# Six places instead of four for w2 groups, and loads five groups ahead, in the last MLP quarter

## The chip, the cores and the metric

The kernel runs on one core of a Trainium2 chip. The metric is the device time of one execution in microseconds; lower is better. The core has TensorE (PE; its weight loads are shown as PEld), VectorE (DVE), ScalarE (ACT), GpSimd (POOL) and SyncE (SP). SyncE and GpSimd issue the DMAs, which all run on the core's 16 DMA engines.

## The reference

The reference computes a transformer-like block and the gradients of all its inputs but one. For x of 2048 tokens by 1024 (bf16):

```python
h = layernorm(x) * (1 + ca) + sa
x = x + ga * spectral(h)              # rfft2, times complex weights, irfft2
h = layernorm(x) * (1 + cb) + sb
y = layernorm(h)
z = y @ w1 + b1                       # 1024 x 3584
x = x + gb * (gelu(z) @ w2 + b2)      # w2: 3584 x 1024
# outputs: x, and by vjp with grad_out the gradients of
# A_x, A_w_r, A_w_i, B_w1, B_b1, B_w2, B_b2, c, w_mod
```

sa to gb are six rows of silu(c) @ w_mod. The change touches only how w2 is brought on chip for `gelu(z) @ w2` on the last 512 tokens.

## The kernel before, in words

The program goes through these stages: modulation rows and the transposed gradient gBoT; the product ph of that gradient with w2 transposed; the forward spectral stage; the MLP forward with its activation's derivative, in four quarters of 512 tokens (b = 0 to 3, some 330 to 768 us); then the pg passes (gz times w1 transposed), the layer norms backward with the gradient of w2, the backward spectral stage, and the gradient of w1.

Within a quarter two kinds of work alternate, in the order of a written list (`plan`):

- `z_block` (seven groups g per quarter, 512 hidden units each): 32 matmuls for z (L802), then ScalarE and VectorE make gelu(z), called hh, and the derivative. The derivative is multiplied into a tile `ph` that was loaded from memory (L796). The product, gz, is stored from that same tile to `d_gz` by GpSimd (L824). Two tiles take turns as `ph`, by the group's running number n: `uvp1[:, 1]` for even n and `uvp2[:, 0]` for odd n. The profile calls these tiles hhC and w2sA. The last z group has n = 27.
- `bo_pass` (two halves h of 512 output columns, seven groups g each): a bias row (L840), then 16 matmuls (L851) per group that add hh times a w2 group into four PSUM banks. The w2 group is 512 KB, and its number is n = (2b + h) * 7 + g, 0 to 55. The last quarter has groups 42 to 55. After the seventh group ScalarE empties the banks into `otile` (L860), VectorE multiplies and adds, and the half is stored to the output.

The z groups of one quarter run beside the `bo` groups of the quarter before, so the last quarter's `bo` groups have no z work beside them.

The w2 groups sit in four places, group n in `w2p[n % 4]`. By their names in the profile the four are w2sA (the second half of that tile, `uvp2[:, 1]`), w2sC, w2sD (the first half, beside the accumulator `gacc`) and w2sB. `w2_load(upto)` issues on SyncE all loads up to a number (L833). In the last quarter it is called with n + 3.

The half's store of the output, `store_tok_half`, is one plain DMA on SyncE (L155) and two indirect scatters on GpSimd (L160). `load_tok_half` brings grad_out for the half by one plain DMA (L137) and two gathers on GpSimd (L142).

While the last `bo` groups run, SyncE also issues what the pg passes need: 28 DMA transposes of w1 into `w1T` (L935) and seven loads of gz into `gzr` (L925). Both are tied behind certain w2 loads by `behind_w2(k)`, which names group 42 + k. The tiles of the next stage, n3u and n2u (L1094, L1096), reuse the memory of `uvp1` and `uvp2`.

A scheduler orders each engine's instructions when the program is built. Orders written with `ordered()` and `tc.issue_after` are kept, and the rest goes by priority and readiness as it estimates them. On the chip each queue then runs in that fixed order, with waits on semaphores. A DMA that writes a tile waits for all that still read or write that part of it.

Of the kernel before, what the change touches and what calls it, by code (L numbers as in the profile page):

```python
# [24 lines left out]
KH = D // 2  # L25
# [5 lines left out]
NB = 4  # L31
# [4 lines left out]
def kernel(  # L36
# [24 lines left out]
    nc = tc.nc  # L61
# [58 lines left out]
    def chunk_rows(dt, i):  # L120
        return dt[4 * i * P:4 * (i + 1) * P, :].rearrange("(q p) d -> p q d", p=P)
# [13 lines left out]
    def load_tok_half(t4, src, i, h):  # L135
        s3 = tok_flat(src)
        nc.sync.dma_start(out=t4[:, 0:4:3, :],  # L137
                          in_=bass.AP(tensor=s3.tensor, offset=s3.offset + 128 * i * D + h * KH, ap=[[D, P], [1024 * D, 2], [1, KH]]))
        s2 = s3.rearrange("n (h d) -> (n h) d", h=2)
        for q in range(2):  # L140
            k = 4 * i + 2 * q + h
            nc.gpsimd.indirect_dma_start(out=t4[:, 1 + q, :], out_offset=None, in_=s2,  # L142
                                         in_offset=bass.IndirectOffsetOnAxis(ap=oidx[:, k:k + 1], axis=0))
# [9 lines left out]
    def store_tok_half(dst, t4, i, h):  # L153
        s3 = tok_flat(dst)
        nc.sync.dma_start(out=bass.AP(tensor=s3.tensor, offset=s3.offset + 128 * i * D + h * KH, ap=[[D, P], [1024 * D, 2], [1, KH]]),  # L155
                          in_=t4[:, 0:4:3, :])
        s2 = s3.rearrange("n (h d) -> (n h) d", h=2)
        for q in range(2):
            k = 4 * i + 2 * q + h
            nc.gpsimd.indirect_dma_start(out=s2, out_offset=bass.IndirectOffsetOnAxis(ap=oidx[:, k:k + 1], axis=0),  # L160
                                         in_=t4[:, 1 + q, :], in_offset=None)
# [7 lines left out]
    def bcn(row, n):  # L169
        return bass.AP(tensor=row.tensor, offset=row.offset, ap=[row.ap[0], [0, n], row.ap[1]])  # L170

    def tt(out, a, b, op):
        return nc.vector.tensor_tensor(out=out, in0=a, in1=b, op=op)  # L173
# [501 lines left out]
    def ordered():  # L675
        return tc.issue_after(last_pe[0].ins)
# [84 lines left out]
    uvp1 = reg.tile([P, 2, 4, BW], BF16, name="hhC", tag="uv1")  # L761
    uvp2 = reg.tile([P, 2, 4, BW], BF16, name="w2sA", tag="uv2")
# [4 lines left out]
    w2p = [uvp2[:, 1], reg.tile([P, 4, BW], BF16, name="w2sC", tag="gm")[:], px1t[:, 0]]  # L767
# [58 lines left out]
    w2_v = B_w2.rearrange("(c p) d -> p c d", p=P)  # L826
    w2_in = []

    def w2_load(upto):
        while len(w2_in) <= min(upto, NB * 14 - 1):  # L830
            n = len(w2_in)
            h, g = n // 7 % 2, n % 7
            w2_in.append(nc.sync.dma_start(out=w2p[n % 4], in_=w2_v[:, g * 4:(g + 1) * 4, h * KH:(h + 1) * KH]))  # L833

    def bo_pass(b, h):
        cs_ = slice(h * KH, (h + 1) * KH)
        pbs = [((ps_s, ps_d)[k % 2] if (b, h) == (NB - 1, 0) else ps_f)("pbo") for k in range(4)]
        for i in range(4):
            with ordered():
                last_pe[0] = nc.tensor.matmul(pbs[i][:], lhsT=ones_bf[32 * i:32 * i + 1, :],  # L840
                                              rhs=b2_row[32 * i:32 * i + 1, cs_], start=True, stop=False,
                                              tile_position=(32 * i, 0))
        for g in range(7):
            n = (2 * b + h) * 7 + g
            w2_load(n + 3 if b == NB - 1 else n)
            wp = w2p[n % 4]
            hh = hh_slots[(b * 7 + g) % 11]
            for i in range(4):
                for k in range(4):
                    with ordered():  # L850
                        last_pe[0] = nc.tensor.matmul(pbs[i][:], lhsT=hh[:, k, i * P:(i + 1) * P], rhs=wp[:, k, :],  # L851
                                                      start=False, stop=(g == 6 and k == 3))
            if g < 6:
                yield
        bo, x1t, go = (otile[0][:, k] for k in range(3))
        nc.sync.dma_start(out=x1t, in_=chunk_rows(d_x1, b)[:, :, cs_])
        load_tok_half(go, grad_out, b, h)
        for i in range(4):
            with tc.high_priority():
                last_ev[0] = nc.scalar.copy(out=bo[:, i, :], in_=pbs[i][:])  # L860
        tt(go, go, bo, ALU.mult)
        tt(bo, bo, bcn(gb_row[:, cs_], 4), ALU.mult)
        tt(bo, bo, x1t, ALU.add)
        store_tok_half(out_0, bo, b, h)

        yield
        pa = (ps_f if (b, h) in ((NB - 2, 1), (NB - 1, 1)) else ps_d)("pa")
        for i in range(4):
            with ordered():
                last_pe[0] = nc.tensor.matmul(pa[32 * i:32 * (i + 1), :], lhsT=ones_bf[:, 0:32], rhs=go[:, i, :], start=True, stop=True)  # L870
        with tc.high_priority():
            if b == 0:
                nc.vector.tensor_copy(out=gacc[:, cs_], in_=pa[:])
            else:
                tt(gacc[:, cs_], gacc[:, cs_], pa[:], ALU.add)

    def bo_both(b):
        for h in range(2):
            late = bo_pass(b, h)
            for _ in range(7):  # L880
                next(late)
                yield
            bo_late.append(late)
# [469 lines left out]
```

## Time and profile before

| | |
|---|---|
| median of three runs | 1469.18 us (1469.07 to 1473.41) |
| the profiled execution's own time | 1474.63 us |
| its span in the profile | 1472.8 us |
| TensorE busy | 1395.1 us, 95% |
| VectorE, ScalarE, GpSimd busy | 1072.9, 717.8, 376.5 us |
| mean granted TensorE clock | 0.988 |
| DMA | 324.27 MB, mean 220 GB/s |
| last quarter's `bo` groups on TensorE | 711.8 to 768.0 us |

Busy time is what an engine's own instructions took; idle time before an instruction is shown in brackets with what ended it. SPq and POOLq rows are issues: a DMA's row there is the time that the queue took to issue it, not the transfer. A timeline row merges neighbours of one line. Where the text gives a landing, it is the last increment of that DMA's completion semaphore in the trace.

### The profile page before, as it was taken

Reading aid. Unit: us, or ns where it says so; the run is one execution under the profiler, and the core shown is the slowest. Engines: PE = TensorE matmul, PEld = TensorE weight load, DVE = VectorE, ACT = ScalarE, POOL = GpSimd, SP = SyncE. Lnnn points to the kernel's source line nnn. Section 1 sums busy time; section 2 is a strip of 40 time slices with the busy share of each in tenths; the row PEclk is TensorE's granted clock in tenths of the full one; section 3 lists DMA queues with packets and bytes.
Section 4 is the critical chain, followed back from the end, with each engine's and each line's share of the span. In section 5 each row is a group of like instructions: output and inputs, shape, how many; then the busy total and the mean of one; then the engine's idle time right before and its main releaser. Section 6 shows DMA issues by size and latency. Waiting matters only on the chain. (4 is left out here: it accounts for less than half of the span.)

```text
span 1472.8 us, 18265 instructions
## 1 busy us (share of the span) xinstructions
PE 1395.1 (95%) x6703; PEld 650.6 (44%) x6835; DVE 1072.9 (73%) x1581; ACT 717.8 (49%) x953; POOL 376.5 (26%) x441
## 2 busy tenths in 40 slices
PE   5889989999999999999989999999999999999997
PEld 2434545444444444444434444444444444444443
DVE  5984786898799788887520789888467578898542
ACT  4765545857887666665312333342622434444211
POOL 5720541211112222122211011021245431322422
PEclk9999999999999999999999999999999999999999
DMA  9982563999777776796999275396699998766993
GB/s 335 279 228 58 144 219 114 262 258 335 242 245 232 235 248 223 229 292 216 235 303 250 91 256 186 121 266 172 184 226 242 236 218 220 191 193 181 291 235 115
DMA packets 358366, 324.27 MB, mean 220 GB/s; under 512 B 209386, under 2 KB 301056, under 8 KB 358022
## 3 DMA queue, kind: packets, MB, share of 16 engines
q1 hardware_dynamic: 324166, 207.71, 52.9%
q0 software_dynamic: 34112, 115.41, 22.8%
q8 instruction: 53, 0.87, 0.2%
q14 instruction: 35, 0.29, 0.1%
HBM read 162.06 MB, written 111.20 MB: 186 GB/s over the span
## 5 line engine op out<-in xcount | busy, mean ns | idle before, releaser
L684 PE MATMUL pp<-gBoT,wt 128*128 128x512 bf16 x878 | 196.8, 381 | 5.8 <-DMA wt<-in_B_w_dram 3.2
L948 PE MATMUL pg<-w1T,gzr 128*128 128x512 bf16 x876 | 194.6, 379 | 1.6 <-ACT gn3a L956 0.2
L1252 PE MATMUL gw1acc<-gzh,n3n 128*128 128x512 bf16 x876 | 193.8, 379 | 2.3 <-DMA gzh<-d_gz 1.3
L802 PEld LDWEIGHTS <-w 128*128 128x128 bf16 x896 | 87.6, 98 | 112.5 <-issue 9.0
L684 PEld LDWEIGHTS <-wt 128*128 128x128 bf16 x896 | 87.7, 98 | 109.9 <-issue 4.2
L948 PEld LDWEIGHTS <-gzr 128*128 128x128 bf16 x896 | 86.8, 98 | 107.9 <-issue 4.9
L1252 PEld LDWEIGHTS <-n3n 128*128 128x128 bf16 x896 | 87.5, 98 | 106.1 <-issue 2.8
L802 PE MATMUL pz<-n3Ta,w 128*128 128x512 bf16 x437 | 99.4, 383 | 6.1 <-ACT gt L805 4.1
L1071 PE MATMUL gw2acc<-gB,hhsA 128*128 128x512 bf16 x438 | 99.3, 384 | 3.7 <-ACT gwo L1078 3.1
L802 PE MATMUL pz<-n3Tb,w 128*128 128x512 bf16 x439 | 98.4, 379 | 0.5
L851 PEld LDWEIGHTS <-hhA 128*128 128x128 bf16 x608 | 59.4, 98 | 77.5 <-issue 8.0
L811 ACT ACTIVATE gt<-gt 128x2048 bf16<-128x2048 bf16 x28 | 53.5, 1911 | 71.1 <-DVE gt L173 71.1
L805 ACT ACTIVATE gt<-pz,b_col 128x512 bf16<-128x512 f32 x112 | 72.8, 684 | 28.9 <-PE pz L802 26.9
L173 DVE TENSOR_TENSOR gt<-gt,gt 128x2048 bf16<-128x2048 bf16 x56 | 68.5, 1223 | 21.6 <-ACT gt L813 20.9
L1256 ACT CAST gwo<-gw1acc 128x512 bf16<-128x512 f32 x50 | 29.0, 584 | 113.0 <-PE gw1acc L1252 98.7
L1078 ACT CAST gwo<-gw2acc 128x512 bf16<-128x512 f32 x46 | 26.8, 584 | 111.7 <-PE gw2acc L1071 84.0
L173 DVE TENSOR_TENSOR ct<-ct 128x2048 bf16<-128x2048 bf16 x64 | 75.9, 1217 | 2.6 <-DMA d_n<-ct 1.8
L992 DVE CUSTOM_DVE_ANT_0 otl<-otl 128x1024 bf16<-128x1024 bf16 x24 | 29.0, 1222 | 57.5 <-DMA otl<-in_w_mod_dram 51.5
L1071 PEld LDWEIGHTS <-hhsA 128*128 128x128 bf16 x448 | 44.1, 99 | 56.4 <-DMA hhsA<-d_hh 3.6
L807 ACT ACTIVATE gt<-gt 128x2048 bf16<-128x2048 bf16 x28 | 53.4, 1908 | 0.6
L813 ACT ACTIVATE gt<-gt 128x2048 bf16<-128x2048 bf16 x28 | 53.4, 1907 | 0.5
L1257 POOL DMA_DIRECT2D out_dram<-gwo x56 | 30.9, 553 | 78.9 <-ACT gwo L1256 46.8
(317 smaller groups left out, 2520.1 us busy)
## 6 DMA issues: line engine op xcount, KB each, us to landing
gzr<-d_gz SPq DMA_DIRECT2D x28, 512.0 KB
wblk<-in_w_mod_dram SPq DMA_DIRECT2D x12, 1024.0 KB
out_dram<-otl POOLq DMA_DIRECT2D x48, 256.0 KB
out_dram<-gwo POOLq DMA_DIRECT2D x96, 128.0 KB
d_ph<-pho POOLq DMA_DIRECT2D x21, 512.0 KB
d_hh<-hhA POOLq DMA_DIRECT2D x19, 512.0 KB
w2sD<-in_B_w_dram SPq DMA_DIRECT2D x14, 512.0 KB
hhC<-d_ph SPq DMA_DIRECT2D x14, 512.0 KB
```

The costliest lines, as they stand in the source:

```text
L173: return nc.vector.tensor_tensor(out=out, in0=a, in1=b, op=op)
L684: last_pe[0] = nc.tensor.matmul(pp[:], lhsT=wt[:, fg % 2, cch, k * P:(k + 1) * P], rhs=gBoT[j][:, cch, :], start=(cch == 0), stop=(cch == ...
L802: last_pe[0] = nc.tensor.matmul(pz[:], lhsT=w1s[g][:, cch, k * P:(k + 1) * P], rhs=n3T[:, cch, :], start=(cch == 0), stop=(cch == NDC - 1))
L805: nc.scalar.activation(out=zb[:, k, :], in_=pz[:], func=ACT.Identity, bias=b1_col[:, fc:fc + 1], scale=1.0)
L807: nc.scalar.activation(out=av, in_=zb, func=ACT.Square)
L811: nc.scalar.activation(out=sg, in_=bv, func=ACT.Sigmoid, scale=2.0 * GK)
L813: nc.scalar.activation(out=bv, in_=bv, func=ACT.Sigmoid, scale=-2.0 * GK)
L851: last_pe[0] = nc.tensor.matmul(pbs[i][:], lhsT=hh[:, k, i * P:(i + 1) * P], rhs=wp[:, k, :], start=False, stop=(g == 6 and k == 3))
L948: last_pg[0] = nc.tensor.matmul(pgs[i][:], lhsT=gzs[b, g][:, k, i * P:(i + 1) * P], rhs=w1Ts[g][:, k, h * KH:(h + 1) * KH], start=(g == 0 ...
L1071: nc.tensor.matmul(acc[:], lhsT=hh_of(fc)[:, t, :], rhs=gBs[t // 4][:, t % 4, h * KH:(h + 1) * KH], start=(t == 0), stop=(t == NT - 1))
L1252: nc.tensor.matmul(acc[:], lhsT=n3ns[t // 4][:, t % 4, cch * P:(cch + 1) * P], rhs=gz2[t // 8][:, t % 8, :], start=(t == 0), stop=(t == NT ...
L1257: nc.gpsimd.dma_start(out=out_4[cch * P:(cch + 1) * P, fg * 512:(fg + 1) * 512], in_=ob)
```

## The change

From group 46 on (the fifth of the last quarter), the w2 groups go round six places instead of four: `uvp1[:, 1]`, `uvp2[:, 0]` and the four old ones in the order w2sD, w2sB, w2sA's second half, w2sC. So 46 and 52 are in hhC's second half, 47 and 53 in w2sA's first half, 48 and 54 in w2sD, 49 and 55 in w2sB, 50 in w2sA's second half, 51 in w2sC. The loads of the last quarter are called for with n + 3 up to n = 44 and with n + 5 from n = 45 on. All other lines are the same; those below the first edit have numbers higher by 8 in the changed kernel.

```diff
     w2_v = B_w2.rearrange("(c p) d -> p c d", p=P)
     w2_in = []
 
+    W2_LAST = (NB - 1) * 14 + 4
+
+    def w2_slot(n):
+        if n < W2_LAST:
+            return w2p[n % 4]
+        k = (n - W2_LAST) % 6
+        return (uvp1[:, 1], uvp2[:, 0])[k] if k < 2 else w2p[(W2_LAST + k - 2) % 4]
+
     def w2_load(upto):
         while len(w2_in) <= min(upto, NB * 14 - 1):
             n = len(w2_in)
             h, g = n // 7 % 2, n % 7
-            w2_in.append(nc.sync.dma_start(out=w2p[n % 4], in_=w2_v[:, g * 4:(g + 1) * 4, h * KH:(h + 1) * KH]))
+            w2_in.append(nc.sync.dma_start(out=w2_slot(n), in_=w2_v[:, g * 4:(g + 1) * 4, h * KH:(h + 1) * KH]))
...
         for g in range(7):
             n = (2 * b + h) * 7 + g
-            w2_load(n + 3 if b == NB - 1 else n)
-            wp = w2p[n % 4]
+            w2_load(n + (5 if n >= W2_LAST - 1 else 3) if b == NB - 1 else n)
+            wp = w2_slot(n)
             hh = hh_slots[(b * 7 + g) % 11]
```

## The prediction

> **What bounds the kernel now.** I read the page's engine line first, then TensorE's timeline in the last MLP quarter, then the queues of SyncE and GpSimd over the same stretch.
>
> ```profile
> PE 1395.1 (95%) x6703; PEld 650.6 (44%) x6835; DVE 1072.9 (73%) x1581; ACT 717.8 (49%) x953; POOL 376.5 (26%) x441
> ```
>
> TensorE is busy 95% of 1472.8 us, so a microsecond taken from or given to its in-order stream mostly reaches the end. In the timeline (start, us, engine, line, out<-in, count, idle before) the last quarter has two waits for a w2 group:
>
> ```profile
> 722.90 3.62 PE L851 MATMUL pbo<-w2sC,hhC 128*128 128x512 bf16 x16
> 726.36 3.62 PE L851 MATMUL pbo<-w2sD,hhA 128*128 128x512 bf16 x16
> 729.81 3.62 PE L851 MATMUL pbo<-w2sB,hhA 128*128 128x512 bf16 x15
> 734.19 3.61 PE L851 MATMUL pbo<-w2sA,hhA 128*128 128x512 bf16 x16 [0.76 <-DMA w2sA<-in_B_w_dram]
> ...
> 742.08 4.90 PE L851 MATMUL pbo<-w2sC,hhA 128*128 128x512 bf16 x16 [3.95 <-DMA w2sC<-in_B_w_dram]
> 746.82 3.62 PE L851 MATMUL pbo<-w2sD,hhB 128*128 128x512 bf16 x15
> ```
>
> These rows are groups 45 to 50 in order (45 starts at 722.90; 46, 47, 48, 49, 50 follow; the bias row before 49 is left out). Groups 48 and 49 wait 0.76 and 3.95 us. Group 49 also runs 4.90 us where 3.62 is usual, because the granted clock is half for 3.41 us there. The change can win 0.76 + 3.95 + 1.28 = 6.0 us, and no more: no other group of this quarter waits.
>
> Why they are late: SyncE issues the load of 48 at 724.40 and of 49 at 730.05, and they land 9.8 and 12.0 us later (last completion increment in the trace at 734.15 and 742.04), where a quiet one takes 3.6 (708.42 to 712.00). The windows (PE busy, PEld, DVE, ACT, POOL, clock, DMA share, GB/s) show all 16 DMA engines full:
>
> ```profile
> 725.00:730.00 5.00, 5.00 (x25) 2.25 (x23) 0.52 (x4) 0.00 (x0) 1.12 (x2) 1.00 1.14 195
> 730.00:735.00 5.00, 4.18 (x19) 1.84 (x19) 0.00 (x0) 0.00 (x0) 0.21 (x1) 1.00 1.17 206
> 740.00:745.00 5.00, 2.92 (x8) 1.08 (x8) 0.84 (x1) 1.07 (x2) 0.00 (x0) 0.66 1.18 265
> ```
>
> The last view is GpSimd's timeline, which the two new places bring into play:
>
> ```profile
> 710.19 0.75 POOL L824 DMA_DIRECT2D d_gz<-hhC  x1 [6.71 <-DVE gb_acc L822]
> ...
> 724.02 1.30 POOL L160 DMA_INDIRECT out_dram<-otile,xu  x1 [1.04 <-DMA out_dram<-otile]
> 725.37 0.80 POOL L824 DMA_DIRECT2D d_gz<-w2sA  x1
> 734.79 0.99 POOL L160 DMA_INDIRECT out_dram<-otile,xu  x1 [8.63 <-issue]
> ```
>
> L824 stores gz out of the two ph buffers, hhC's second half and w2sA's first half, which become the new places. The 8.63 us before the second scatter are a wait: GpSimd holds a semaphore instruction of 8.69 us there until the first scatter, issued at 724.02, has landed at 734.01 (10.0 us). Both write the output, so the second waits for the first. Whatever stands behind the second scatter in that queue waits too.
>
> **The change, part by part.**
>
> *Issuing five ahead instead of three.* The same 14 loads of 512 KB, the same matmuls; VectorE's and ScalarE's orders are unchanged, TensorE's too but for the places read. Nothing is added in work. On a DMA system that is full from 710 to 790 us, earlier loads push other transfers back: at 714 one load more is in flight than before, worth 512 KB at some 200 to 260 GB/s, 2 to 2.6 us of all other traffic.
>
> *Group 46 into hhC.* It must wait for the gz store issued at 710.19, which lands at 714.34. So it is issued at about 714.4 and lands by 720 at the neighbours' latency (4.4 to 5.4 us); it is needed at 726.4. Cost nothing; cover 6 us.
>
> *Group 47 into w2sA's first half.* This decides. That half is ph of the very last z group; VectorE finishes it at 725.1 and GpSimd stores it. In the built program the orders around it are (numbers are w2 groups, T a w1 transpose):
>
> ```
> SyncE  before: 44 T 45 T 46 T out x1 47 go T 48 T gz 49 T 50 T 51 ...
> SyncE  after:  44 T 45 46 T T 48 out x1 49 go T 50 T T gz 47 51 52 T ...
> GpSimd before: gather gather scatter1 gz-store scatter2
> GpSimd after:  gather gather scatter1 scatter2 gz-store
> ```
>
> Two steps are moved. On SyncE, 47 now stands behind 48, 49 and 50, and with it 51, 52 and the transposes stand behind 47's wait. On GpSimd the gz store has gone behind the second scatter. So 47's load hangs on a chain: scatter 1 lands, scatter 2 is issued, the gz store is issued, lands, the load is issued, lands. TensorE needs group 47 at 729.8 and its order is fixed, so all of the chain past 729.8 is idle time.
>
> The chain with this run's rows: scatter 1 is still issued at 724.0 and lands at 734.0. Scatter 2 follows at 734.8 as it did, and takes 1.0 us to issue, so the store is issued at 735.8 instead of 725.4. From 734.0 to 742.96 the software queue moved the rest of the store (4.5 us, landed at 738.50) and then scatter 2 (4.46 us); after the change it has the two in the other order, and I give them the same 8.9 us: 734.8 + 8.9 = 743.7. The store's own latency is bounded by 3.35 us (the one issued at 695.95) and 13.13 us (the one issued at 725.37); mine is 7.9, between them, by the queue it shares. SyncE has reached the wait by then: two transposes and a gz load after 724.4 took until 738.6 here (issue times of 4.31, 0.56 and 7.26 us).
>
> The load: 4.42 to 5.81 us for those issued between 738 and 749, 3.45 in a quiet stretch (673.45), 12.0 at worst (730.05). SyncE has issued nothing for some microseconds, so I take 4.5, near the lower rows. Group 47 lands at 748.2.
>
> By a formula of the Trainium skill (DMA: Bandwidth & Descriptors, Anatomy of one DMA) a 512 KB transfer takes 2.0 us plus its bytes at 436 GB/s, an estimate of 3.2 us. The quiet rows of 3.35 and 3.45 agree; the 13.13 and 12.0 of this stretch do not. By it store and load would end at 742.2 and the net cost be some 7.7 us.
>
> *Sum.* Idle before group 47: 748.2 - 729.8 = 18.4. One half-clock stretch after it: 1.3, as at 742 (the longest such stretch in the trace, 6.83 us, would cost 3.4; no idle time this long has a row). Given back: 6.0, since 48, 49 and 50 are in their places by then. Net 18.4 + 1.3 - 6.0 = +13.7 us.
>
> *What is late next.* Nothing. From 748.2 group 47 ends at 753.0, 48 at 756.5, and 51 starts at 764.1, 53 at 771, 54 at 774.4, 55 at 777.9. 51 and 52 are issued right behind 47 and land by 752. 53 to 55 find their places free at 753.0, 756.5 and 760.3, and 55 is issued at about 762, behind an output store that needs VectorE's three operations of half 0. With 6 us each, all have 9 us or more to spare. The pg pass starts at 781 instead of 768, and what it loads has had 13 us more to arrive; it did not wait before. From 768 to 1125 TensorE waits for no DMA, only for VectorE and ScalarE, which follow it (1.2 us at most, 2.8 in all), so the shift is neither enlarged nor absorbed.
>
> The profiled execution took 1474.63 us (span 1472.8 and 1.8 around it) against a median of 1469.18; I add the difference to each: 1488.3 for such a profile, 1482.9 for the median.
>
> **Rivals.**
>
> *Early landing, a gain.* If the gz store landed by 726, 47 would be in place and the change would win its 6.0 us: 1463.2. It decides from 734.5 on: a landing of the load before that is a net gain. For it: most scatters and stores outside this stretch take 2.4 to 4.4 us. Against it: with the fastest row of each step, scatter 1 lands at 724.0 + 2.4 = 726.4, the store is issued at 728.2 and lands at 731.6, the load at 735.0, still a net +0.5. And the 16 engines were full. The Trainium skill (Trainium Kernel Development and Optimization, Best Practices) asks for double-buffering so that DMA overlaps compute, which speaks for this rival. The row of 8.69 us shows why more places need not give it: a queue stands at a wait. A sentence of the skill (DMA: Bandwidth & Descriptors, Anatomy of one DMA), that semaphore waits happen on the issuing sequencer and not in the DMA engines, agrees with that row, and speaks against this change. Chance 4%.
>
> *A short stall.* DMA engines empty while SyncE stands, scatter 1 lands at 730, store and load at quiet latency: 731.8 + 3.4 + 3.5 = 738.7, but SyncE must also be there in time. Idle 8.9, net +4.2: 1473.4, about no change. Chance 8%.
>
> *A longer stall.* The one load more delays scatter 1 by 2 us, the store takes its 13.13 again and the load 8: 737.8 + 13.1 + 8 = 758.9, idle 29.1, net +24.4: 1493.6. Against it: what contended with that store, the transposes, is held behind 47 now. Chance 12%.
>
> *The change does not do what it says* in part already: "five ahead" holds for the program's text, but 47 is issued after 50. If later work had slack for the 13.7 us, the time would stay at 1469. The 95% speaks against it; it belongs to the 8%.
>
> **How the numbers follow.** The long wait of the forecast has 76%. Its own range: landing of 47 between 742 and 755, so idle 12 to 25 and net +7.5 to +20.5, 1476.7 to 1489.7. The range given is widened to the short and longer stalls: 1474 to 1492, about 84%. A measurement of this kernel tells 0.3% (4.4 us) from no change: the gain (4%) is faster; most of the short stall (8%) is the same; forecast and longer stall are slower (88%).
>
> **What would show it.** Right: TensorE idle of 12 to 25 us before the group after 46, put down to a DMA into w2sA; GpSimd's gz store issued after 734; SyncE idle in front of that load; no wait at 48 and 49; pg starting at about 781. Wrong: that group waits under 5 us, or the store is issued before 728; or the idle is there and the span does not grow; or a second wait at 51 to 55.

## The result, and the profile after

| | before | changed |
|---|---|---|
| median of six runs | 1469.12 us (1467.18 to 1475.54) | 1484.02 us (1480.65 to 1487.66) |
| profiled execution, its span | 1474.63, 1472.8 us | 1480.65, 1478.9 us |
| last quarter, first bias row to first pg matmul | 56.2 us | 66.1 us |
| TensorE's waits in that quarter | 4.7 us | 13.5 us |
| clock granted at half in that quarter | 3.4 us | 13.7 us |

The ratio of the runs is 1.0085 (1.0063 to 1.0107): the change costs about 12.5 us (9.3 to 15.7). The medians alone lie 14.9 us apart, inside that interval. The forecast was +13.7.

The engine line of the page of the changed kernel has the same work in a longer span:

```profile
PE 1394.0 (94%) x6703; PEld 652.3 (44%) x6835; DVE 1073.1 (73%) x1581; ACT 718.4 (49%) x953; POOL 374.5 (25%) x441
```

TensorE's timeline of the changed kernel in the last quarter (start, us, engine, line, out<-in, count, idle before):

```profile
724.31 3.62 PE L859 MATMUL pbo<-hhC,hhA 128*128 128x512 bf16 x16
741.25 3.17 PE L859 MATMUL pbo<-w2sA,hhA 128*128 128x512 bf16 x7 [13.31 <-DMA w2sA<-in_B_w_dram]
744.63 2.90 PE L859 MATMUL pbo<-w2sA,hhA 128*128 128x512 bf16 x8 [0.22 <-issue]
747.37 3.62 PE L859 MATMUL pbo<-w2sD,hhA 128*128 128x512 bf16 x16
...
775.86 7.07 PE L956 MATMUL pg<-w1T,gzr 128*128 128x512 bf16 x31
```

Group 46 starts out of hhC without a wait. Group 47 waits 13.31 us for the load into w2sA (TensorE had run dry at 727.94) and then takes 6.12 us (741.25 to 747.37) where 3.46 is usual. Group 48 and all that follow to the pg pass wait for nothing, so the two waits of the profile before are gone.

GpSimd's and SyncE's timelines of the changed kernel show who held that load (SPq rows are issues):

```profile
726.09 1.00 POOL L160 DMA_INDIRECT out_dram<-otile,xu  x1 [5.15 <-DMA out_dram<-otile]
732.31 1.00 POOL L160 DMA_INDIRECT out_dram<-otile,xu  x1 [5.23 <-issue]
733.32 0.81 POOL L824 DMA_DIRECT2D d_gz<-w2sA  x1
```

```profile
726.52 0.53 SPq L841 DMA_DIRECT2D w2sA<-in_B_w_dram  x1
727.11 4.60 SPq L943 DMA_TRANSPOSE w1T<-in_B_w_dram  x2
731.82 0.52 SPq L933 DMA_DIRECT2D gzr<-d_gz  x1
737.83 0.37 SPq L841 DMA_DIRECT2D w2sA<-in_B_w_dram  x1
```

The first scatter, issued at 726.09, lands at 731.52; the second follows at 732.31, and only behind it the gz store at 733.32. The store lands at 737.78. SyncE has stood since 732.34 and issues the load of 47 at 737.83, 0.05 us after that landing. It lands at 741.20, and TensorE starts at 741.25. (The row at 726.52 is group 50, in the other half of the same tile.) Every link of the forecast's chain is there.

The windows of the changed kernel (PE busy, PEld, DVE, ACT, POOL, clock, DMA share, GB/s) show how busy the DMA engines were meanwhile, and the clock:

```profile
730.00:735.00 5.00, 0.00 (x0) 0.00 (x0) 0.00 (x0) 0.00 (x0) 1.81 (x2) 0.80 1.06 275
735.00:740.00 5.00, 0.00 (x0) 0.00 (x0) 0.00 (x0) 0.00 (x0) 0.00 (x0) 0.50 0.61 215
740.00:745.00 5.00, 3.53 (x8) 1.31 (x10) 0.00 (x0) 0.00 (x0) 0.00 (x0) 0.50 1.06 306
```

While SyncE stands, the DMA share drops to 0.61. And the clock is at half from 733.0 to 746.7, through the idle time and 5.4 us past its end.

### The profile page after: what moved, and what is told of

It reads as the page before. It is cut to its first block, busy times and chain, and to the rows that moved or that the text cites. A ratio compares the mean times of both kernels' runs of the same rounds, so it can differ in the third digit from the quotient of the medians.

```text
span 1478.9 us, 18260 instructions
## 1 busy us (share of the span) xinstructions
PE 1394.0 (94%) x6703; PEld 652.3 (44%) x6835; DVE 1073.1 (73%) x1581; ACT 718.4 (49%) x953; POOL 374.5 (25%) x441
## 5 line engine op out<-in xcount | busy, mean ns | idle before, releaser
L811 ACT ACTIVATE gt<-gt 128x2048 bf16<-128x2048 bf16 x28 | 53.5, 1910 | 69.8 <-DVE gt L173 69.8
L173 DVE TENSOR_TENSOR otile<-otile 128x2048 bf16<-128x2048 bf16 x16 | 19.5, 1220 | 45.6 <-ACT otile L868 45.4
```

The lines of the kernel that those rows point to most:

```text
L811: nc.scalar.activation(out=sg, in_=bv, func=ACT.Sigmoid, scale=2.0 * GK)
```

## The experiments

**Theory.** Group 47's place is free only once the last gz store, queued behind a scatter that waits for another scatter, has landed; that costs all of the time. **Rivals.** The idle is due to the lead of five groups (loads pushed together on a full DMA system); or to the store's place in GpSimd's queue alone; or to SyncE, which reaches the load late anyway.

The medians of the kernel before, run on the same chips, are 1472.46 (lead_three, gz_ahead, five_places, w2sa_sixth), 1473.22 (gz_between, w2sa_third, five_places_late_w1T) and 1468.96 (gz_ahead_late_w1T). Ratios are against these runs.

**1. Six places, lead of three** (lead_three).

```diff
-            w2_load(n + (5 if n >= W2_LAST - 1 else 3) if b == NB - 1 else n)
+            w2_load(n + 3 if b == NB - 1 else n)
```

> Six places as in the change, but the loads are called for three groups ahead again. In the built program all five queues have the very order of the changed kernel, so the theory (the place of group 47 waits for the last gz store, whatever the lead) expects the changed kernel's time again: about 1484 us, 12 to 17 us over the kernel before, and one idle stretch of 12 to 18 us before group 47. If issuing five ahead was what crowded the DMA engines (rival), the time goes back to about 1469.

Ratio 1.0082 (1.0053 to 1.0110). TensorE's timeline:

```profile
743.75 3.17 PE L859 MATMUL pbo<-w2sA,hhA 128*128 128x512 bf16 x7 [14.02 <-DMA w2sA<-in_B_w_dram]
```

The same wait and the same loss, as expected. The scheduler had put all queues of this kernel and of the changed one in the same order: the lead written in the program moves nothing, and all of the cost belongs to the places. So this run is the changed kernel a second time. It can't tell whether loads that go out earlier crowd the DMA engines; experiment 7 can.

**2. The last gz store ahead of both scatters** (gz_ahead).

```diff
-            nc.gpsimd.indirect_dma_start(out=s2, ...
+            with tc.issue_after(gz_in[0].ins) if (i, h) == (NB - 2, 1) else ExitStack():
+                nc.gpsimd.indirect_dma_start(out=s2, ...
...
-            nc.gpsimd.dma_start(out=d_gz_v[...], in_=ph)
+            gz_in[0] = nc.gpsimd.dma_start(out=d_gz_v[...], in_=ph)
```

> The changed kernel, but GpSimd issues the last gz store ahead of both scatters of the third quarter's second half. Theory: the store is issued when VectorE is done, at about 723 instead of 733.3; it lands behind the two gathers of its queue at about 731, SyncE gets to the load at about 732, the load lands at 736. So the idle time before group 47 falls from 13.3 to about 8 us, the half-clock time after it by about 1, and the median to about 1478. Rival (the DMA engines are simply full, the queue's order does not matter): idle stays at 13 and the time at 1484.

Ratio 1.0069 (1.0047 to 1.0091); the wait for 47 is 9.95 us where about 8 was expected. TensorE's, GpSimd's and SyncE's timelines of this kernel:

```profile
738.64 3.17 PE L862 MATMUL pbo<-w2sA,hhA 128*128 128x512 bf16 x7 [9.95 <-DMA w2sA<-in_B_w_dram]
```

```profile
724.09 0.80 POOL L827 DMA_DIRECT2D d_gz<-w2sA  x1 [2.40 <-DVE gb L1032]
```

```profile
728.33 5.52 SPq L946 DMA_TRANSPOSE w1T<-in_B_w_dram  x2
733.96 0.52 SPq L844 DMA_DIRECT2D w2sA<-in_B_w_dram  x1
```

The store is issued 9 us earlier than in the changed kernel (724.09 against 733.32) and lands at 730.95, after 6.86 us. But group 46 ends at 728.7, so the store alone is too late already; and SyncE is busy issuing two transposes until 733.9. The load goes out 3.0 us after the place is free and lands at 738.60. The store's place in GpSimd's queue explains a part of the idle, not all of it. The shorter wait does not show in the total: the median is 1484.28 where about 1478 was expected, and the interval overlaps the changed kernel's.

**3. The store between the two scatters** (gz_between): as 2, with the condition `(i, h, q) == (NB - 2, 1, 1)`, so that only the second scatter goes behind the store.

> The changed kernel with GpSimd's order of the kernel before: scatter 1, gz store, scatter 2. If the second scatter's place was the whole cause, the store is issued some 6 us sooner and the idle time falls from 13.3 to about 7. Theory, by the software queue's order: the store's data still follow scatter 1, which lands at 731.5, by 4 to 4.5 us, so it lands at about 736 instead of 737.8 and the idle time is 11 to 12; the median 1 to 2 us under the changed kernel's.

Ratio 1.0085 (1.0052 to 1.0119). TensorE's and GpSimd's timelines:

```profile
738.92 5.30 PE L862 MATMUL pbo<-w2sA,hhA 128*128 128x512 bf16 x16 [8.74 <-DMA w2sA<-in_B_w_dram]
```

```profile
726.75 0.99 POOL L163 DMA_INDIRECT out_dram<-otile,xu  x1 [3.58 <-DMA out_dram<-otile]
727.75 0.80 POOL L827 DMA_DIRECT2D d_gz<-w2sA  x1
733.53 0.99 POOL L163 DMA_INDIRECT out_dram<-otile,xu  x1 [4.98 <-issue]
```

The wait is 8.74 us, between the theory's 11 to 12 and the 7 of the rival, nearer the rival. The store lands at 734.25, 1.5 us after scatter 1 at 732.75, and its latency of 6.50 us is no longer than that of the stores ahead of both scatters (6.86 in 2, 6.96 in 4). So sharing the software queue with one scatter costs it little; what costs is standing behind the second. The wait is 4.6 us shorter than in the changed kernel, but the total does not show it (1 to 2 us less were expected). The two intervals overlap widely, so that says neither that the gain was there nor that it was lost.

**4. Store ahead, and the w1 transposes three groups later** (gz_ahead_late_w1T): as 2, and `behind_w2(fc - 5)` for `behind_w2(fc - 8)`.

> The last gz store ahead of both scatters, as in the earlier run, and the w1 transposes tied three w2 loads later. There the store had landed at 730.95, but SyncE, behind transposes, issued the load of 47 only at 733.96, and it landed at 738.6. Theory: SyncE's queue was the second gate; with less in it the load is issued when the store lands, about 730 to 731, lands at 734 to 735, and the idle time falls from 9.95 to 5 to 7 us. Rival (the queue was no gate): idle stays near 10.

Ratio 1.0045 (1.0016 to 1.0075). TensorE's and SyncE's timelines:

```profile
737.47 4.95 PE L862 MATMUL pbo<-w2sA,hhA 128*128 128x512 bf16 x15 [6.97 <-DMA w2sA<-in_B_w_dram]
```

```profile
726.06 6.34 SPq L946 DMA_TRANSPOSE w1T<-in_B_w_dram  x2
732.89 0.37 SPq L844 DMA_DIRECT2D w2sA<-in_B_w_dram  x1
```

SyncE now issues the load 0.05 us after the store's landing at 732.84, as in the changed kernel, and 6.97 us of wait are left, at the edge of the 5 to 7 expected. The store was issued at 725.88, took 6.96 us, and the load 4.53. With both queues out of the way these two transfers in a row still end 7 us after TensorE needs the group. No order of the queues that was tried makes this place good enough for the second group of the ring.

**5. The same half as third place** (w2sa_third): group 48 is the first in it, lead four.

```diff
-        return (uvp1[:, 1], uvp2[:, 0])[k] if k < 2 else w2p[(W2_LAST + k - 2) % 4]
+        return (uvp1[:, 1], w2p[2], uvp2[:, 0], w2p[3], w2p[0], w2p[1])[k]
```

> Six places, with w2sA's first half as the third of the ring: group 48 is the first in it. Theory: the load's landing is set by the store's chain alone (741 where group 46 ends at 727.8), so each step down the ring takes one group of 3.46 us off the idle time: 13.3 becomes about 9.9 before group 48 and the quarter some 62.7 us; the median falls by about 3.5 us from the changed kernel's. Rival (six places' loads crowd the engines): idle of 13 stays, or splits over groups 47 to 49.

Ratio 1.0077 (1.0047 to 1.0107). TensorE's timeline:

```profile
732.41 3.62 PE L859 MATMUL pbo<-w2sD,hhA 128*128 128x512 bf16 x16
745.86 6.26 PE L859 MATMUL pbo<-w2sA,hhA 128*128 128x512 bf16 x16 [9.83 <-DMA w2sA<-in_B_w_dram]
```

The wait goes with the place to group 48 and is 3.48 us shorter than 13.31: one group of 3.46 us. Expected was 9.9. The store landed at 742.08, the load at 745.81. Counted from the quarter's first bias row that is 31.4 us for the load, and 31.5 in the changed kernel: the chain is fixed in time, and the ring decides only how much work stands ahead of it. The total does not show the shorter wait here either; the intervals overlap.

**6. The same half as sixth place** (w2sa_sixth): group 51 is the first in it, lead four.

```diff
-        return (uvp1[:, 1], uvp2[:, 0])[k] if k < 2 else w2p[(W2_LAST + k - 2) % 4]
+        return (uvp1[:, 1], uvp2[:, 0])[k // 5] if k % 5 == 0 else w2p[(W2_LAST + k - 1) % 4]
```

> Six places, but w2sA's first half is the sixth of the ring instead of the second: group 51 is the first to use it. Theory: the gz store lands at about 738 and the load at about 741 to 744; group 51 is needed at 742 (727.8 and four groups of 3.46 us and two short rows later), so the idle time before it is 0 to 2 us and the median 1463 to 1471. Rival (crowding by six places' loads): 1478 or more, with the wait at 47 to 49.

Ratio 1.0036 (1.0016 to 1.0056), a miss: the wait was 1.30 us, within the 0 to 2 expected, and the quarter took 52.3 us, but the median is 1478.34 where 1463 to 1471 was expected. TensorE's timeline:

```profile
745.95 3.61 PE L859 MATMUL pbo<-w2sA,hhB 128*128 128x512 bf16 x16 [1.30 <-DMA w2sA<-in_B_w_dram]
...
774.33 0.62 PE L878 MATMUL pa<-otile,ones_bf 128*32 128x512 bf16 x4 [3.18 <-DVE otile L173]
```

In this profile the wait has moved. The plain store of the output half stands on SyncE behind the load of 51 and transposes, and is issued at 754.70 (748.68 in experiment 8). Its scatters follow, ScalarE empties the last banks only at 771.95, once the second scatter has landed (771.85), and TensorE waits 3.18 us for what VectorE makes of them, with 3.4 us at half clock from 773.85. No other profile has a wait there. That this is what the total lost is argued from one profile, not shown.

**7. Five places, without that half** (five_places), lead four.

```diff
-        k = (n - W2_LAST) % 6
-        return (uvp1[:, 1], uvp2[:, 0])[k] if k < 2 else w2p[(W2_LAST + k - 2) % 4]
+        k = (n - W2_LAST) % 5
+        return uvp1[:, 1] if k < 1 else w2p[(W2_LAST + k - 1) % 4]
```

> Five places from group 46 on: hhC's second half and the four old ones, four ahead; w2sA's first half is not used. Theory: no load waits for the last gz store, so the long idle stretch is gone; groups 48 and 49 find places one group sooner than in the kernel before, so of its 6.0 us some or all is won: 1463 to 1469. Rival (more loads in flight crowd the DMA engines): waits of several microseconds stay and the time is 1475 or more.

Ratio 1.0002 (0.9981 to 1.0022). TensorE's timeline:

```profile
727.40 3.62 PE L859 MATMUL pbo<-hhC,hhA 128*128 128x512 bf16 x16
730.86 3.62 PE L859 MATMUL pbo<-w2sD,hhA 128*128 128x512 bf16 x15
...
742.41 3.61 PE L859 MATMUL pbo<-w2sC,hhB 128*128 128x512 bf16 x15 [0.60 <-DMA w2sC<-in_B_w_dram]
...
757.83 3.61 PE L859 MATMUL pbo<-w2sA,hhA 128*128 128x512 bf16 x16 [0.47 <-DMA w2sA<-in_B_w_dram]
```

Group 47 now comes out of w2sD and waits for nothing; with one wait of 0.33 us for VectorE, the waits of the quarter are 1.4 us. Up to the stall the loads go out at much the same times as in the changed kernel (2.7, 8.7, 11.8 and 17.3 us into the quarter; there 2.6, 8.9, 10.6 and 16.8), so crowding by them is out as the cause. With that one place taken away all of the slowdown is gone. The gain over the kernel before (1463 to 1469 was expected, the median is 1476.16) did not show.

**8. Five places, and the w1 transposes three groups later** (five_places_late_w1T): as 7, with the edit of the transposes from 4.

> Five places (hhC's second half and the four old ones) as in the earlier run, and the w1 transposes tied behind w2 loads three groups later than now, so that fewer of them are in flight beside the w2 loads. If DMA in the last quarter is what the kernel before loses there: waits in the quarter under 1 us in all, 50 to 51 us for it (51.9 with five places alone, 56.2 in the kernel before), and the median 1464 to 1470. Rival (VectorE, which lags in the later stages, takes back what TensorE wins here): the quarter is as short, the time within 0.2% of the kernel before.

Ratio 1.0000 (0.9983 to 1.0018). No group of the quarter waits any more: it takes 50.1 us, from which the others below can be built up. As a total it is not told apart from the kernel before: 1472.82 us, where 1464 to 1470 was expected. It was the best candidate for a version faster than both, and it is not shown to be one. A short quarter and an unchanged total are what the rival (VectorE takes back later what TensorE wins here) said; no run tests whether VectorE is the reason.

**9 and 10. The kernel before, profiled twice more** (before_again, before_third).

> The kernel before, profiled a second time. Its first profile took 1474.63 us against medians of 1469.1 and 1472.5, so its waits before groups 48 and 49 may not be typical. If they are a property of the program: waits of 4 to 5 us again, and 56 us from the last quarter's first bias row to the pg pass. If that run was unlucky: 50 to 53 us for the quarter, and then the change costs 13 to 16 us there and not 10.

> The kernel before, profiled a third time, for the spread of its own waits: 56.2 and 52.9 us for the last quarter so far. Between 52 and 57 us if these are its bounds. The later part, from the pg pass to TensorE's last matmul, took 696.8 and 702.9 us; if TensorE's shift is partly taken back there, it stays over the changed kernel's 695.2 and 698.6.

TensorE's timeline of the first and of the second:

```profile
742.93 3.61 PE L851 MATMUL pbo<-w2sC,hhA 128*128 128x512 bf16 x16 [2.88 <-DMA w2sC<-in_B_w_dram]
```

```profile
737.36 3.61 PE L851 MATMUL pbo<-w2sC,hhA 128*128 128x512 bf16 x16 [1.22 <-DMA w2sC<-in_B_w_dram]
```

Group 48 waits in neither, group 49 2.88 and 1.22 us instead of 3.95, and no clock is lost. The load of 49 took 9.3 and 8.4 us there against 12.0 in the profile that the prediction read. The quarters took 52.9 and 51.3 us; the second lies under the 52 to 57 expected.

**All profiles side by side** (us; a quarter is 50.1 of work, plus its waits, plus a rest, which is mostly what half clock adds to the work):

| kernel | waits | rest | quarter | from there to TensorE's end |
|---|---|---|---|---|
| before, three profiles | 4.7, 2.9, 1.2 | 1.4, 0, 0 | 56.2, 52.9, 51.3 | 696.8, 702.9, 704.0 |
| changed | 13.5 | 2.5 | 66.1 | 695.2 |
| lead_three | 14.2 | 2.0 | 66.4 | 698.6 |
| gz_ahead | 10.2 | 2.2 | 62.5 | 697.7 |
| gz_between | 8.7 | 1.7 | 60.6 | 701.4 |
| w2sa_third | 9.8 | 2.7 | 62.6 | 694.6 |
| gz_ahead_late_w1T | 7.0 | 1.4 | 58.5 | 700.8 |
| w2sa_sixth | 1.8 | 0.3 | 52.3 | 702.8 |
| five_places | 1.4 | 0.4 | 51.9 | 704.5 |
| five_places_late_w1T | 0 | 0 | 50.1 | 696.6 |

The rest is what is left of the quarter after 50.1 and the waits. In w2sa_sixth and five_places no stretch at half clock lies in the quarter, and what their 0.3 and 0.4 us are stays open.

## Why the prediction was right, point by point

- **46 in hhC costs nothing.** Right: its load lands at 718.56, needed at 724.31.
- **47 waits for a chain that ends with the gz store.** Right, link by link. Taking that place away removes the slowdown (7); moving it one step down the ring takes one group's time off the wait (5).
- **"Earlier loads push other transfers back."** Not seen as a cost: with the lead of three the order of all queues is the same (1), and with five places and a lead of four no slowdown is left (7). The prediction read the built order of the queues for 47, but not that the called-for lead had no effect on it at all.
- **Scatter 1 lands 10.0 us after its issue.** Mis-sized: 5.43. It was issued 2 us later in the span, and 4 us later within a quarter that began 2 us earlier, because the plain store ahead of it landed only at 725.25. The two errors nearly cancel, by luck: the store's issue came 5.4 us after TensorE ran dry (733.32 against 727.94), forecast 6.0 (735.8 against 729.8).
- **The store's latency, 7.9 us.** Mis-sized, the largest error in the wait: 4.46. **The load's, 4.5:** 3.37. The prediction gave scatter 2 and the store 8.9 us together in the software queue; they took 5.5 (732.31 to 737.78). In the four profiles where SyncE stood and held the transposes, the store took 3.89 to 5.89 us and the load 3.37 to 4.11 (changed kernel, 1, 5, 6). In the three where SyncE went on issuing transposes they took 6.50 to 6.96 and 4.53 to 4.63 (2, 3, 4). That the transposes make the difference is argued from this, not tested alone. The prediction named this relief as an argument against a longer stall and took the load near its lower rows for it, but gave the store nothing for it. Issue, store and load together (0.6 + 3.4 + 1.1) make the 5.1 us by which the wait came out shorter than 18.4. The formula of the Trainium skill that the prediction cited (DMA: Bandwidth & Descriptors, Anatomy of one DMA), by which 512 KB are an estimate of 3.2 us, stands there for DMAs that GpSimd issues. The store is one, and its 4.46 lies above it; the load, which SyncE issues, took 3.37, near it.
- **Half clock after the wait, 1.3 us.** Mis-sized: group 47 lost 2.66 us (0.22 of it a pause), twice that, since 5.4 us of its work ran at half clock. The row of before that the prediction took had 0.77 us of idle time inside its half-clock stretch.
- **Given back, 6.0 us.** The mechanism is right (48 and 49 do not wait), the size was one profile's. In three profiles the kernel before loses 6.1, 2.8 and 1.2 us there (quarter less 50.1), a mean of 3.4. With the measured terms the sum is 13.5 + 2.5 - 3.4 = +12.6, beside the 12.5 (9.3 to 15.7) of the ratio; that the two are so near is less sure than it looks, with one profile on one side and three on the other. The forecast's 13.7 came that close partly by luck: its wait was too long by 5 us, its half clock too short by 1.2, and what it gave back too large by 2.6.
- **Nothing late next.** Right: no group from 48 to 55 waits, and pg starts 66.1 us into the quarter.
- **The signs.** The idle of 13.31 us, SyncE idle in front of that load, and no wait at 48 and 49 came as named. Three times were off: the store was issued at 733.32 and not after 734, group 47 landed at 741.20 and not between 742 and 755, and pg started at 775.86 and not at 781. The quarter began 2.0 us earlier in this profile; but for that the first two would have come as named, and pg some 3 us early.
- **"The shift is neither enlarged nor absorbed."** Not settled. The sum for the quarter and the ratio agree for the changed kernel, but the last column of the table spreads over 10 us. It is 694.6 to 698.6 in the four profiles with the longest quarters and 696.6 to 704.5 in the five with the shortest, as if a part were taken back later; the three profiles of the kernel before alone spread over 7 us, so that is not shown. The same spread is why the shorter quarters of 7 and 8 (1.6 and 3.4 us under the mean of before, 53.5) can't be found in the totals; whether and where they are lost later stays open.

Of the rivals, the early landing and the short stall are out; the chain came 5 us earlier than forecast, part of the way to the short stall, and stayed inside the forecast's own 12 to 25 us of idle.

## What to carry to other kernels

Before a buffer gets a second use, look up who reads it last, and what stands ahead of that reader in its queue: here the last reader was a DMA store behind two scatters on another engine, and a place that comes free 10 us after it is needed is worse than no place. Leaving that place out was enough here (1.0002). Put last in the ring it still cost 0.36%, so look at what its load's wait holds up in its own queue. Read the built order of the queues before pricing a lead written in the program, and profile a DMA wait more than once before counting it as a gain.

## What the runs showed of the hardware that was not expected

- The same DMA wait of the same program was 3.95, 2.88 and 1.22 us in three profiles; the 512 KB load behind it took 12.0, 9.3 and 8.4 us, and a load of the same size 3.37 in the changed kernel, where its queue had stood for 5.5 us.
- All half-clock stretches of the last quarter were 3.41 us or two, three or four times that (3.41 in the first profile of before; 6.83 in 3 and 4, 10.24 in 2 and 5, 13.65 in the changed kernel and 1).
- After 13.3 us of idle TensorE worked 5.4 us at half clock, at 427 ns from one matmul to the next where 216 is usual. By the Trainium skill (TensorE: Matmul & The Clock Gate, What's actually happening) full speed returns only after a busy window of some 3.4 us, and the windows run on by themselves, so that part of one more may be lost. An estimate by that is 3.4 to 6.8 us at half clock, a cost of 1.7 to 3.4; the 5.4 us here lie in it. Two other stretches do not: after its wait TensorE worked only 2.64 us at half clock in the first profile of the kernel before (742.08 to 744.72) and 2.71 in experiment 4 (737.47 to 740.18), so here less than the 3.4 us was enough.
